# A threshold attention feeding a gated feed-forward: GpSimd's order in the lead-in, a later copy, and output pieces in the last slot

## The chip, the cores and the metric

The kernel runs on one core of a Trainium2 chip. The metric is the device time of one execution in microseconds; the median of three runs counts. The core has a tensor engine (PE, with its weight loads shown as PEld), a vector engine (DVE), a scalar engine (ACT), GpSimd (POOL) and a sync engine (SP). Each works through its own queue in order. SP, ACT and POOL can also issue DMA transfers.

## What is computed

```
# q, k, v: 8 images x 8 heads x 576 rows x 64
scores = q @ k.T / sqrt(64)
thresh = max(scores) - tau                      # per row, tau = 0.02
scores = where(scores >= thresh, scores, -1e9)
attn   = exp(scores - max(scores)); attn /= sum(attn) + 1e-9
x      = (attn @ v), heads side by side         # 4608 x 512
h      = x @ w_in                               # 512 -> 2048
g      = h * clip(h + 3, 0, 6) / 6
out    = g @ w_out                              # 2048 -> 512
```

## The kernel before

**Slots.** The attention is cut into 144 slots, 18 per image. A slot is 128 query rows of one pair of heads; slot numbers run through all images. For each slot:

- PE computes the scores of two slots at once in a `burst` (line 203), into the score columns of PSUM (`score_col`, line 196: banks 0 to 5; odd slots use banks 0 and 1, and 3 and 4, even slots 1 and 2, and 4 and 5). A burst can write only where the maxima of the two slots before have been read.
- DVE copies the scores to SBUF and takes the row maximum, one instruction per head (`sm_max`, line 225, instruction at line 233).
- POOL turns the maximum into a bias (`sm_bias`, line 241): one two-head instruction per slot, except in slots 0 and 1, where each head has its own.
- ACT applies the threshold (`sm_mask`, line 245, needs the bias) and the exponential with its row sum (`sm_exp`, line 250).
- DVE inverts the sum (`sm_recip`), POOL normalises into bf16 (`sm_norm`, line 257, two instructions per slot). This frees the slot's score tile in SBUF; there are five such tiles.
- The result is transposed on PE for the first ten slots (`pe_transpose`, with copies out by DVE, lines 281 and 282), and by DMA from SP for the others.

**Products and feed-forward.** `multiply(n)` (line 401) gives the products with v that are due in slot n and returns their copies out of PSUM (line 297, into `xT`; line 306, into `xR`). When the four products of a chunk are there, its feed-forward items go into the list `todo1`. An item (`mm1`, line 314) multiplies with `w_in`; then comes r = max(h + 3, 0) on ACT or DVE (lines 330 and 332) and the gate g on DVE (line 345). There are two r tiles. When a chunk's last item has been taken, its output tiles go into `todo2`, four pieces to a tile (`mm2_part`, line 352, four blocks of `w_out` each). A finished tile is copied out (`mm2_out`, line 359) and stored by four DMAs.

**The order.** It is written out by hand. The lead-in (`for n in range(0, N1, 2)`, line 476) takes slots 0 to 13 two at a time. One cycle issues: copies of the transposes, the burst for n + 2 and n + 3, the norms of the two slots before, the maximum of n + 2, the products with their copies, transposes, then the loads of slots n and n + 1 (`issues`), the maximum of n + 3, and ACT's exponentials and masks. In cycle n = 0 the loads of slot 0 are issued earlier, around the maximum of slot 2. The lists `issues` (lines 417 to 448) say which load is issued in which slot: pieces of `w_in` in 0, 0, 1, 1 and of `w_out` in 4, 6, 8, 10, all by POOL; slot 1 also has the k load of quad 2, by SP.

The main loop (line 518) takes slots 14 to 143 one at a time. In odd slots from 21 on `second()` (line 465) issues two pieces of an output tile on PE into bank 7 (`OB`), but not in the last slot, 143. Then the drain: `rest1` takes the items left, in banks 0, 3, 2, 5 in turn; `rest2` takes the pieces left, with banks 6 and 7 and copies out by ACT and DVE in turn (`count`); `last_tile` (line 571) does the last output tile in two halves with DMAs of their own.

What matters for the change: in cycle n = 12 the product copied is the fourth of the first chunk, and slot 14's item reads all four. The bias of a slot stands on POOL behind everything that was issued on POOL before it.

Of the kernel before, what the change touches and what calls it, by code (L numbers as in the profile page):

```python
# [20 lines left out]
def kernel(  # L21
# [10 lines left out]
    nc = tc.nc  # L32
# [7 lines left out]
    N1, N2 = 14, 21  # L40
    HB, OB = 6, 7
# [31 lines left out]
    issues = {}  # L73
    jobs = {}

    def at(when, n, job):
        when.setdefault(n, []).append(job)
# [90 lines left out]
    now = -1  # L168
# [14 lines left out]
    queue = []  # L183
    for b in range(B):
        for g, t in ((0, 0), (0, 1), (1, 0), (1, 1), (None, 4), (0, 2), (0, 3), (1, 2), (1, 3)):
            for i in range(2):
                sl = Slot()
# [8 lines left out]
    def score_col(n, a):  # L196
        return (512 - OWN if n % 2 else 1024 - P) + 1536 * a
# [27 lines left out]
    def sm_max(sl):  # L225
        sl.s = s_pool.tile([P, 2, S], F32, tag="s", name="s")
        sl.m = stat_pool.tile([P, 2], F32, tag="m", name="m")
        sl.bias = stat_pool.tile([P, 2], F32, tag="bias", name="bias")
        sl.rsum = stat_pool.tile([P, 2], F32, tag="rsum", name="rsum")
        sl.rinv = stat_pool.tile([P, 2], F32, tag="rinv", name="rinv")  # L230
        for i in range(2):
            c0 = score_col(sl.n, i)
            nc.vector.tensor_scalar(out=sl.s[:, i, :], in0=ps_flat[:, c0:c0 + S],  # L233
                                    scalar1=1.0, scalar2=None, op0=Alu.mult, op1=Alu.max,
                                    accum_out=sl.m[:, i:i + 1])
            if sl.n < 2:
                sm_bias(sl, slice(i, i + 1))
        if sl.n >= 2:
            sm_bias(sl)

    def sm_bias(sl, of=slice(0, 2)):
        nc.gpsimd.tensor_scalar(out=sl.bias[:, of], in0=sl.m[:, of], scalar1=-scale, scalar2=tau, op0=Alu.mult,  # L242
                                op1=Alu.add)
# [10 lines left out]
    def sm_recip(sl):  # L254
        nc.vector.reciprocal(out=sl.rinv[:], in_=sl.rsum[:])  # L255
# [18 lines left out]
    def pe_transpose(sl):  # L274
        i = sl.n % 2
        most = ps[:, (OB, HB)[i], :].bitcast(BF16).rearrange("p (c t) -> p c t", t=P)
        one = ps_flat[:, 1472 + 1536 * i:1536 + 1536 * i].bitcast(BF16)
        pn = sl.pn[:].rearrange("p a b -> p (a b)")
        for c in range(9):
            nc.tensor.transpose(most[:, c, :] if c < 8 else one, pn[:, c * P:(c + 1) * P], identb[:])  # L280
        return (lambda: nc.vector.tensor_copy(out=sl.dst[:, 8, :], in_=one),
                lambda: nc.vector.tensor_copy(out=sl.dst[:, 0:8, :], in_=most))
# [9 lines left out]
    def av_main(b, hp, chunk):  # L292
        if hp == chunk == 0:
            xT[b] = x_pool.tile([P, KI, 512], BF16, tag="xT", name="xT")
        pb = bank()
        av(pb, b, hp, pts[b, hp, chunk], slice(0, 256))
        return lambda: nc.vector.tensor_copy(out=xT[b][:, hp, 256 * chunk:256 * chunk + 256], in_=pb)  # L297

    def av_rest(b):
        pb = bank()  # L300
        for hp in range(NPAIR):
            av(pb[:, 64 * hp:64 * hp + 64], b, hp, ptr[b, hp % 2], slice(64 * (hp // 2), 64 * (hp // 2) + 64))
        if b % 2 == 0:
            xR[b // 2] = x_pool.tile([P, KI, P], BF16, tag="xR", name="xR")
        o0 = 64 * (b % 2)
        return lambda: nc.vector.tensor_copy(out=xR[b // 2][:, :, o0:o0 + 64],
                                             in_=pb.rearrange("p (a b) -> p a b", a=NPAIR))

    def half_columns(out, lhsT, rhs, start, stop):
        w = 64 if now < len(queue) - 1 else P  # L310
        for c in range(0, P, w):
            nc.tensor.matmul(out[c:c + w], lhsT[:, c:c + w], rhs, start=start, stop=stop)  # L312
# [39 lines left out]
    def mm2_part(mt, part, ob=OB):  # L352
        if part == 0:
            o_ps[0] = ps[:, ob, :]
        for ni in range(part * 4, part * 4 + 4):
            half_columns(o_ps[0], gbuf[:, ni, mt * P:(mt + 1) * P], w_out_sb[:, ni, :],
                         start=(ni == 0), stop=(ni == NI - 1))
# [15 lines left out]
    todo2 = []  # L373
# [7 lines left out]
    def whole(b, chunk):  # L381
        mt = 5 * (b % 2) + 2 * chunk
        items = [((b, ni, 256 * chunk), ()) for ni in range(0, NI, 2)]
        items[-1] = (items[-1][0], [(b // 2, mt + i, part) for i in range(2) for part in range(4)])
        return items

    def odd_items(b, halves):
        items = [((b, ni, None), ()) for half in halves for ni in (8 * half, 8 * half + 4)]
        if 1 in halves:
            items[-1] = (items[-1][0], [(b // 2, 4, part) for part in range(4)])  # L390
        return items
# [9 lines left out]
    def multiply(n):  # L401
        copies = []
        for b, hp, chunk in products.get(n, ()):
            if hp is None:
                copies.append(av_rest(b))
                if b % 2:
                    todo1.extend(odd_items(b, (0,) if b < B - 1 else (0, 1)))
                elif b:
                    todo1.extend(odd_items(b - 1, (1,)))
            else:  # L410
                copies.append(av_main(b, hp, chunk))
                if hp == NPAIR - 1:
                    todo1.extend(whole(b, chunk))
        return copies
# [16 lines left out]
    def v_pieces(b, slots):  # L431
        pieces = []

        def piece(i):
            if not pieces:
                pieces.extend(load_v(b))
            pieces[i]()

        for i, n in enumerate(slots):
            at(issues, n, lambda i=i: piece(i))  # L440

    v_pieces(0, (-1, -1, -1, -1, 0, 0, 0, 0))
    for b in range(1, B):
        v_pieces(b, (13, 14, 15, 16, 17, 18, 19, 20) if b == 1 else [(b - 1) * NSLOT + n for n in range(8, 24, 2)])
    for i, n in enumerate((0, 0, 1, 1)):
        at(issues, n, lambda i=i: load_w_in(i))
    for i, n in enumerate((4, 6, 8, 10)):
        at(issues, n, lambda i=i: load_w_out(i))
# [11 lines left out]
    for i in range(2):  # L460
        sm_max(queue[i])
# [2 lines left out]

    def second():
        nonlocal pieces, bb, mt, part
        pieces = 2 if now % 2 and todo2 and N2 <= now < len(queue) - 1 else 0
        for _ in range(pieces):
            bb, mt, part = todo2.pop(0)
            mm2_part(mt, part)  # L470

    pieces = bb = mt = part = 0
    waiting = [[], []]
# [2 lines left out]
    for n in range(0, N1, 2):  # L476
        now = n
        last = [queue[m] for m in (n - 2, n - 1) if m >= 0]
        ones, most = waiting
        for copy in ones:  # L480
            copy()
        for sl in last:
            sm_recip(sl)
        for copy in most[0:1]:
            copy()
        burst(n + 2, by=nc.sync)
        for copy in most[1:]:
            copy()
        for job in jobs.get(n, ()):
            job()  # L490
        for sl in last:
            sm_norm(sl)
        if n == 0:
            for issue in issues[0][:4]:
                issue()
        sm_max(queue[n + 2])
        if n == 0:
            for issue in issues[0][4:]:
                issue()
        warm_up({0: 15, 2: 8}.get(n, 3))  # L500
        for copy in multiply(n):
            copy()
        copies = [pe_transpose(sl) for sl in last if sl.on_chip]
        waiting = [[c[0] for c in copies], [c[1] for c in copies]]
        for issue in (issues.get(n, []) if n else []) + issues.get(n + 1, []):
            issue()
        sm_max(queue[n + 3])
        for m in (n, n + 1):
            for i in range(2):
                sm_exp(queue[m], i)  # L510
            for i in range(2):
                sm_mask(queue[m + 1], i)
# [5 lines left out]
    for n, sl in enumerate(queue[N1:], N1):  # L518
        now = n
        last = queue[n - 1:n]  # L520
# [33 lines left out]
        if part == 3:  # L554
            outs.append((bb, mt))
            part = 0
# [14 lines left out]
    def last_tile(mt):  # L571
        c = d_model // 2
        for half in range(2):
            o_half, columns = ps[:, (2, 5)[half], 0:c], slice(half * c, half * c + c)
            for ni in range(NI):
                nc.tensor.matmul(o_half, gbuf[:, ni, mt * P:(mt + 1) * P], w_out_sb[:, ni, columns],
                                 start=(ni == 0), stop=(ni == NI - 1))
            osb = o_pool.tile([P, d_model], F32, tag="osb", name="osb")
            nc.vector.tensor_scalar_mul(out=osb[:, 0:c], in0=o_half, scalar1=1.0 / 6.0)
            for i in range(4):  # L580
                (nc.scalar if i % 2 or half == 0 else nc.sync).dma_start(
                    out=rows_of(B - 1, 12 + i)[:, columns], in_=osb[R * i:R * i + R, 0:c])

    def rest1(item, then, on_act=True):
# [25 lines left out]
    now = len(queue)  # L610
# [42 lines left out]
```

## Time and profile before

| | |
|---|---|
| median of three runs | 501.12 us (500.88 to 501.15) |
| profiled execution, its own time | 501.12 us |
| its span | 499.4 us |
| POOL's norms (line 260) | 288, 748 ns each |
| maxima (line 233) | 288, 750 ns each |
| masks and exponentials (lines 247, 252) | 288 each, 763 and 671 ns |
| POOL's bias (line 242) | 146, 189 ns each |
| matmuls with `w_out` (line 312) | 1021, 379 ns each from issue to end |
| `w_in` loads | 4, 512 KB each, 8.8 us to landing |
| granted PE clock | full over almost the whole span |

How to read it: "busy" is time in which an engine had an instruction at work. PE's matmuls overlap, so their mean duration is longer than their distance. The chain that ended last is followed back from the last instruction. A bracket behind a row of the time line gives the engine's idle time before it and what ended it; a wait for several things is put down to the last of them. "x8" means that eight instructions were merged into one row.

### The profile page before, as it was taken

The numbers are of one execution on the slowest core, as the hardware profiler recorded it, in microseconds if no ns is written. First come the engines' busy times: TensorE is split into PE (matmuls) and PEld (weight loads), VectorE is DVE, ScalarE is ACT, GpSimd is POOL, SyncE is SP. The second block draws the span as 40 slices with busy tenths as digits, with TensorE's granted clock in tenths as the row PEclk, the third lists the DMA queues.
The fourth block names the chain that finished last, engine by engine and source line by source line (L and its number), as shares of the span: only waits on it lengthen the run. The fifth ranks groups of instructions, "written<-read, shape, count | busy, mean of one in ns | idle before, by whom it ended". The sixth has DMA issues, their size and how long they took to land.

```text
span 499.4 us, 17393 instructions
## 1 busy us (share of the span) xinstructions
PE 484.4 (97%) x6803; PEld 359.3 (72%) x6807; DVE 446.0 (89%) x1154; ACT 441.5 (88%) x949; POOL 294.1 (59%) x536
## 2 busy tenths in 40 slices
PE   8888999999999999999999999999999999998996
PEld 7767766777677776777677776777777776776474
DVE  6899998999999999999999999999999998887242
ACT  2899999999999999999999999999999999999132
POOL 3877786666666666666666666666666565554000
PEclk9999999999999999999999999999999999999999
DMA  7999998997999889998999798998999877766421
GB/s 213 177 200 190 150 173 168 223 121 165 174 176 190 119 174 184 216 145 176 166 205 178 129 173 179 220 149 154 181 187 191 123 144 116 151 118 118 91 59 42
DMA packets 192627, 79.98 MB, mean 160 GB/s; under 512 B 171169, under 2 KB 183841, under 8 KB 192545
## 3 DMA queue, kind: packets, MB, share of 16 engines
q1 hardware_dynamic: 175216, 55.27, 61.9%
q0 software_dynamic: 16896, 23.07, 24.0%
q8 instruction: 53, 0.87, 0.7%
q10 hardware_dynamic: 432, 0.52, 0.4%
q14 instruction: 30, 0.24, 0.2%
HBM read 36.70 MB, written 9.44 MB: 92 GB/s over the span
## 4 chain that ended last, share of the span: by engine, by line
PE 79%; ACT 12%; DVE 6%; issue 1%; POOL 1%; DMA 0%; SPq 0%; DVEq 0%
PE ps L312 45%; PE ps L219 26%; PE ps L289 6%; ACT s L247 5%; ACT s L252 5%; DVE s L233 4%; ACT r L330 1%; DVE g L345 1%; PE ps L155 1%; POOL w_in_sb L136 1%; DMA out_dram<-osb 0%; POOL pn L260 0%; DVE r L332 0%; DVE osb L364 0%; PE ps L159 0%
## 5 line engine op out<-in xcount | busy, mean ns | idle before, releaser
L260 POOL TENSOR_SCALAR pn<-s,rinv 128x576 bf16<-128x576 f32 x288 | 211.6, 748 | 15.1 <-issue 1.3
L233 DVE TENSOR_SCALAR_CACHE_REDUCE s<-ps 128x576 f32<-128x576 f32 x288 | 205.2, 750 | 16.3 <-PE ps L219 12.9
L247 ACT ACTIVATE s<-s,bias 128x576 f32<-128x576 f32 x288 | 205.8, 763 | 9.4 <-POOL bias L242 9.4
L252 ACT ACTIVATE s<-s 128x576 f32<-128x576 f32 x288 | 192.4, 671 | 0.0
L219 PE MATMUL ps<-kT,qT 32*128 32x128 f32 (+3 forms) x2560 | 167.3, 414 | 4.8 <-DVE s L233 4.4
L219 PEld LDWEIGHTS ps<-kT,qT 32*128 32x128 f32 (+1 forms) x2560 | 124.1, 174 | 49.2 <-DVE s L233 11.1
L312 PE MATMUL ps<-xT,w_in_sb 128*64 128x256 bf16 (+1 forms) x1936 | 132.9, 274 | 1.4 <-DVE g L345 1.4
L312 PE MATMUL ps<-w_out_sb,g 128*64 128x512 bf16 (+1 forms) x1021 | 130.7, 379 | 0.2
L312 PEld LDWEIGHTS <-w_in_sb 128*64 128x64 bf16 (+1 forms) x1936 | 105.7, 109 | 11.4 <-issue 4.2
L242 POOL TENSOR_SCALAR bias<-m 128x2 f32<-128x2 f32 (+1 forms) x146 | 27.6, 189 | 138.4 <-DVE rinv L255 123.6
L312 PEld LDWEIGHTS <-g 128*64 128x64 bf16 (+1 forms) x1024 | 61.6, 109 | 48.1 <-issue 0.2
L345 DVE SCALAR_TENSOR_TENSOR g<-r,ps 128x512 bf16<-128x512 f32 x128 | 87.4, 684 | 8.3 <-ACT r L330 4.4
L330 ACT ACTIVATE r<-ps,three 128x512 f32<-128x512 f32 x81 | 55.2, 686 | 25.4 <-PE ps L312 24.5
L252 ACT ACTIVATION_READ_ACCUMULATOR s<-s 128x1 f32 x288 | 54.8, 190 | 0.0
L289 PEld LDWEIGHTS <-v 128*64 128x64 bf16 x960 | 41.4, 111 | 16.0 <-issue 3.6
L289 PE MATMUL ps<-pT,v 128*64 128x256 bf16 x640 | 45.4, 273 | 1.6 <-DVE s L233 1.5
L332 DVE TENSOR_SCALAR r<-ps 128x512 f32<-128x512 f32 x63 | 43.3, 688 | 0.4
L119 POOL DMA_DIRECT2D v<-in_v_dram x64 | 36.9, 578 | 9.2 <-DVE kT L110 4.8
L364 DVE TENSOR_SCALAR osb<-ps 128x512 f32<-128x512 f32 x32 | 21.9, 684 | 8.5 <-PE ps L312 8.5
L297 DVE CAST xT<-ps 128x256 bf16<-128x256 f32 x64 | 26.0, 406 | 3.8 <-PE ps L289 3.4
L110 DVE STREAM_TRANSPOSE kT<-nk 128x320 f32<-128x320 f32 (+1 forms) x64 | 26.3, 451 | 0.9 <-DMA nk<-in_k_dram 0.9
L96 DVE STREAM_TRANSPOSE qT<-nq 128x640 f32<-128x640 f32 (+2 forms) x33 | 24.6, 749 | 0.6 <-DMA nq<-in_q_dram 0.6
(35 smaller groups left out, 173.5 us busy)
## 6 DMA issues: line engine op xcount, KB each, us to landing
out_dram<-osb SPq DMA_DIRECT2D x140, 64.0 KB, 2.5
nk<-in_k_dram POOLq DMA_DIRECT2D x12, 576.0 KB, 4.8
nq<-in_q_dram POOLq DMA_DIRECT2D x12, 576.0 KB, 4.9
v<-in_v_dram POOLq DMA_DIRECT2D x32, 80.0 KB, 4.1
v<-in_v_dram POOLq DMA_DIRECT2D x32, 64.0 KB, 3.1
w_in_sb<-in_moe_w_in_dram POOLq DMA_DIRECT2D x4, 512.0 KB, 8.8
w_out_sb<-in_moe_w_out_dram POOLq DMA_DIRECT2D x4, 512.0 KB, 7.0
pT<-pn SPq DMA_TRANSPOSE x120, 4.4
```

What stands on the lines that cost most here:

```text
L119: nc.gpsimd.dma_start(out=vsb[b % 2][32 * g:32 * g + 32].rearrange("p (hp a) c -> p a hp c", a=2)[:, a, :, c0 * D:(c0 + count) * D], in_=v ...
L219: mm = nc.tensor.matmul(ps_flat[rows, c0:c0 + w], qT[c:c + 32, j, q0:q0 + rows.stop - rows.start], kT[c:c + 32, j, k0:k0 + w], start=(j == ...
L233: nc.vector.tensor_scalar(out=sl.s[:, i, :], in0=ps_flat[:, c0:c0 + S], scalar1=1.0, scalar2=None, op0=Alu.mult, op1=Alu.max, accum_out=sl ...
L242: nc.gpsimd.tensor_scalar(out=sl.bias[:, of], in0=sl.m[:, of], scalar1=-scale, scalar2=tau, op0=Alu.mult, op1=Alu.add)
L247: nc.scalar.activation(out=s, in_=s, func=Act.Prelu, bias=sl.bias[:, i:i + 1], scale=scale, alpha=REJECT)
L252: nc.scalar.activation(out=s, in_=s, func=Act.Exp, accum_out=sl.rsum[:, i:i + 1])
L260: nc.gpsimd.tensor_scalar(out=pn[:, i, :], in0=sl.s[:, i, :], scalar1=sl.rinv[:, i:i + 1], scalar2=1.0, op0=Alu.mult, op1=Alu.mult)
L289: nc.tensor.matmul(pb[a * 64:(a + 1) * 64, :], vsb[b % 2][:, 2 * hp + a, u * D:(u + 1) * D], pT[:, block, cols], start=(c == 0), stop=(c = ...
L312: nc.tensor.matmul(out[c:c + w], lhsT[:, c:c + w], rhs, start=start, stop=stop)
L330: nc.scalar.activation(out=r, in_=hps, func=Act.Relu, bias=three[:])
L332: nc.vector.tensor_scalar(out=r, in0=hps, scalar1=3.0, scalar2=0.0, op0=Alu.add, op1=Alu.max)
L345: nc.vector.scalar_tensor_tensor(out=out, in0=r, scalar=6.0, in1=hps, op0=Alu.min, op1=Alu.mult)
```

## The change

Five edits:

1. The pieces of `w_in` are issued with slots 0, 1, 2 and 3, and in cycle n = 0 the loads of slot 1 are issued behind the maximum of slot 3. On POOL the order becomes: bias of slot 2, one piece, bias of slot 3, one piece, norms of slots 0 and 1, bias of slot 4, two pieces, bias of slot 5. The k load of quad 2 on SP moves with the loads of slot 1.
2. Slot 2 has a bias per head.
3. In a lead-in cycle in which no slot is transposed on PE (only n = 12 has both that and a product), the copy of the product comes behind the maximum of slot n + 3.
4. In slot 143 two pieces of the next output tile are issued, into bank 4, one of the score banks. The tile's other two pieces follow in the drain in the same bank. With it `count` starts at 0, so that the copies out of the drain change places between ACT and DVE.
5. Both halves of the last tile issue two DMAs from ACT and two from SP; before, the first half issued all four from ACT.

```diff
@@ sm_max
-            if sl.n < 2:
+            if sl.n < 3:
                 sm_bias(sl, slice(i, i + 1))
-        if sl.n >= 2:
+        if sl.n >= 3:
             sm_bias(sl)
@@
-    for i, n in enumerate((0, 0, 1, 1)):
+    for i, n in enumerate((0, 1, 2, 3)):
         at(issues, n, lambda i=i: load_w_in(i))
@@ second
-        pieces = 2 if now % 2 and todo2 and N2 <= now < len(queue) - 1 else 0
+        pieces = 2 if now % 2 and todo2 and now >= N2 else 0
         for _ in range(pieces):
             bb, mt, part = todo2.pop(0)
-            mm2_part(mt, part)
+            mm2_part(mt, part, ob=OB if now < len(queue) - 1 else 4)
@@ lead-in
-        for copy in multiply(n):
-            copy()
-        copies = [pe_transpose(sl) for sl in last if sl.on_chip]
+        products_out = multiply(n)
+        chip = [sl for sl in last if sl.on_chip]
+        if chip:
+            for copy in products_out:
+                copy()
+        copies = [pe_transpose(sl) for sl in chip]
         waiting = [[c[0] for c in copies], [c[1] for c in copies]]
-        for issue in (issues.get(n, []) if n else []) + issues.get(n + 1, []):
-            issue()
+        if n:
+            for issue in issues.get(n, []) + issues.get(n + 1, []):
+                issue()
         sm_max(queue[n + 3])
+        if n == 0:
+            for issue in issues[1]:
+                issue()
+        if not chip:
+            for copy in products_out:
+                copy()
@@ last_tile
-                (nc.scalar if i % 2 or half == 0 else nc.sync).dma_start(
+                (nc.scalar, nc.sync)[i % 2].dma_start(
```

## The prediction

> **What bounds the kernel now.** I read four views: the page's busy times and chain, the chain in order of time, the time line of the first 76 us, and the time line from 450 us.
>
> ```profile
> PE 484.4 (97%) x6803; PEld 359.3 (72%) x6807; DVE 446.0 (89%) x1154; ACT 441.5 (88%) x949; POOL 294.1 (59%) x536
> ...
> PE 79%; ACT 12%; DVE 6%; issue 1%; POOL 1%; DMA 0%; SPq 0%; DVEq 0%
> ```
>
> TensorE is busy for 484.4 of 499.4 us, and between 200 and 440 us the stretches show it without a gap. So time can come out only where PE idles or where its work can be moved into idle time: the lead-in (before 100 us PE idles 7.6 us) and the end.
>
> In the chain in order of time the lead-in runs through GpSimd:
>
> ```profile
> 14.42 1.44 DVE s L233 x4
> 16.98 2.24 POOL w_in_sb L136 x3
> 19.57 1.49 POOL pn L260 x2
> 21.08 1.46 DVE s L233 x4
> 22.80 1.44 ACT s L247 x2
> ```
>
> The time line says why (columns: start, duration, engine, line; the bracket is idle time and what ended it):
>
> ```profile
> 16.16 1.44 ACT L247 ACTIVATE s<-s,bias 128x576 f32<-128x576 f32 x2 [0.38 <-POOL bias L242]
> 16.18 3.04 POOL L136 DMA_DIRECT2D w_in_sb<-in_moe_w_in_dram  x4
> ...
> 19.51 1.44 ACT L247 ACTIVATE s<-s,bias 128x576 f32<-128x576 f32 x2 [0.59 <-POOL bias L242]
> 19.57 2.92 POOL L260 TENSOR_SCALAR pn<-s,rinv 128x576 bf16<-128x576 f32 x4
> ...
> 22.80 1.44 ACT L247 ACTIVATE s<-s,bias 128x576 f32<-128x576 f32 x2 [0.52 <-POOL bias L242]
> ```
>
> Four weight-load issues (3.04 us, 0.76 each) stand on POOL ahead of the bias of slot 3; the normalisations of slots 0 and 1 come after that, the bias of slot 4 after those. ACT waits 0.38 + 0.59 + 0.52 = 1.49 us.
>
> The next stretch is the hand-over from lead-in to main loop:
>
> ```profile
> 48.63 0.42 DVE L297 CAST xT<-ps 128x256 bf16<-128x256 f32 x1
> ...
> 49.39 1.07 PE L312 MATMUL ps<-xT,w_in_sb 128*64 128x256 bf16 x16
> ...
> 50.39 2.28 PE L219 MATMUL ps<-kT,qT 32*128 32x128 f32 x32
> ...
> 50.78 0.68 DVE L332 TENSOR_SCALAR r<-ps 128x512 f32<-128x512 f32 x1
> ...
> 52.91 0.72 DVE L233 TENSOR_SCALAR_CACHE_REDUCE s<-ps 128x576 f32<-128x576 f32 x1
> ```
>
> From 47.27 to 76.2 us DVE is idle only once (0.22 us at 61.39, waiting for ACT's r). So here DVE sets the pace, and what DVE has gained by slot 16 is what the rest can inherit. The end:
>
> ```profile
> 455.55 1.03 PE L312 MATMUL ps<-xT,w_in_sb 128*128 128x256 bf16 x8 [0.56 <-DVE g L345]
> ...
> 457.45 1.03 PE L312 MATMUL ps<-xT,w_in_sb 128*128 128x256 bf16 x8 [0.87 <-DVE g L345]
> ...
> 461.78 13.98 PE L312 MATMUL ps<-w_out_sb,g 128*128 128x512 bf16 x63
> ...
> 494.30 2.71 ACTq L581 DMA_DIRECT2D out_dram<-osb  x6
> ...
> 496.04 0.79 SPq L581 DMA_DIRECT2D out_dram<-osb  x2
> ```
>
> PE idles 0.56 + 0.87 = 1.43 us for free banks, then runs almost without a gap to 495.55; that run sets the end.
>
> **Part 1, POOL's order in the lead-in (weight loads, bias per head).** Removed: three issues between the biases of slots 2 and 3. Added: one one-head bias (0.19 us, the row at 10.11). By rows: the first head's maximum of slot 2 is done at 15.16, its bias at 15.45, ACT is free at 15.68 (13.01 mask plus 2.67 a slot), so that mask starts 0.48 earlier. Then one issue (16.18 to 16.94); bias of slot 3 behind its maximum (17.19) at 17.29; second issue to 18.26; the four normalisations 18.35 to 21.27; bias of slot 4 to 21.55, its mask at 21.57 instead of 22.80: ACT gains 1.23. The last two issues run to 23.1, bias of slot 5 to 23.36 (not needed before 24.24), and the normalisations of slots 2 and 3 start at 23.46, as before (23.44): they cover nothing and cost nothing. The key load of quad 2, moved with the issues on SP, passes only a no-op that waits for the burst; it was issued at 13.34 and is read at 24.50. The weights are first read at 49.39, and a load lands in 8.8 us (the page), so their lateness costs nothing.
>
> What DVE gains is less. Its maximum of slot 5 waited for the buffer that slot 0's normalisation frees (0.09 us at 21.08), and its copies waited 0.38 for PE transposes behind slot 1's. Freed of both, slot 5's maximum ends at 22.35, the burst for slots 6 and 7 ends at 22.41 + 2.23 = 24.64, and slot 6's maximum starts 0.16 later, at 24.80, instead of 25.34: **0.54 us**. From there the lead-in is a loop of two maxima, one copy and a burst, 5.57 us a cycle (36.13, 41.70, 47.27) against ACT's 5.33, so ACT's lead shrinks to DVE's and 0.54 arrives at slot 14 (46.73).
>
> **Part 2, the later copy.** The xT copy goes behind the maxima of slot 15. Nothing is added on DVE, but this copy is the fourth of the four that the first hidden-layer item reads. Without the shift it would end at 50.40, with it at 49.86, instead of 49.05. PE starts that item at 48.85, runs 6 of 16 matmuls, and then waits until 49.92. Behind it in PE's queue stands the burst for slots 16 and 17, and DVE's r. The 10 left take 10 x 1.0/16 = 0.63, so the burst starts at 50.55 (before: 50.39) and ends at 52.78; slot 16's maximum follows 0.17 later, at **52.95 against 52.91**. The 0.54 is spent, plus 0.04. DVE waits about 0.5 for r meanwhile. ACT still leads by 0.5 to 0.9, which takes the 0.22 at 61.39. Head: 0.54 - 0.58 + 0.22 = **0.18 us**. Bounds: if the wait cost nothing, 0.54 + 0.22 = 0.76; if DVE's 0.54 never came, the copy would end at 50.40, the burst start at 51.09 and slot 16 at 53.49, a loss of 0.58 - 0.22 = 0.36. I take 0.18, since both ends need a row to be wrong.
>
> A rule of the Trainium skill speaks against this part ("PSUM — Partial Sum Buffer", section "Engine vs sequencer instructions"): matmuls start and complete in program order. In this trace PE's weight loads idle 0.74 and 1.04 us around the two waits of 0.56 and 0.87, so nothing ran past them. By the rule the head is 0.18; if the burst could pass the waiting item, 0.76.
>
> **Part 3, two pieces in the last slot.** Eight matmuls of 512 columns, 13.98 / 64 = 0.218 us each, 1.75 us, leave the run at 461.78 and go behind slot 143's item, at about 452.2. Bank 4 was last read by slot 143's maximum, to 450.95: no wait. The next three items then start at 454.0, 454.9 and 455.8 and end before ACT's r reach them (456.01, 456.66, 457.50, with ACT held by the exps to 456.1); the fourth starts at 456.7 (its bank is free at 455.50), the fifth at 457.6 (457.40). So both idle times are filled and the r-g chain isn't late. The xR items end at 461.94 - 1.43 + 1.75 = 462.26, with 1.75 less to follow: **1.43 us** gained. An item alone lasts 1.03, in a row 0.85 to 0.9 (3.50 us for 33 weight loads at 451.31), so up to 0.35 more can come with the restart: 1.78. I take **1.6**. If the pieces delayed the r-g chain after all, this falls towards 0. The copies out change engines (last full tile on DVE, 0.69 instead of ACT's 0.60), off PE's path: the copy after it waits for PE until 495.55.
>
> **Part 4, the last DMAs.** ACT issued six, ending at 497.01; SP's two ended at 496.83. Two and two, behind a copy done at 496.01, end on both at about 496.85: **0.16 us**. SP has the four issues of the tile before (to 494.4) and then two of the first half (to 495.4) ahead, so it is free. Bounds 0 and 0.2.
>
> Sum: 0.18 + 1.6 + 0.16 = 1.94. The profiled execution took 501.12 us (span 499.4 and 1.7 around it), which is also the median. **499.2 us**.
>
> **Rivals.**
> - *The copy's wait is harmless.* For it: DVE has other work just behind the copy (two reciprocals, the xR copy). Against: r and the burst both come behind that item. Head 0.76, total 2.5: 498.6.
> - *The pieces are hidden anyway.* If the tail were set by ACT's r and DVE's g, whose pairs follow each other at 1.50 us from 456.01 to 461.2, filling PE's gap would bring nothing. Against: from 461.78 PE has 34 us of work left and DVE waits 5.3 us for it. 0.18 + 0.16: 500.8.
> - *Slower: a wait that comes back with every image.* In the main loop PE waits for maxima where an image's products change bank (0.36 at 95.50, 0.67 at 102.08), and later no more. If the new phase of DVE against PE brought back about 0.5 us in each of the last six images, 3.0 us would be added: 501.12 - 1.94 + 3.0 = 502.2. It decides from 2.9 us on. Against: everything behind slot 24 moves together.
>
> **How the numbers follow.** Forecast 0.66, harmless copy 0.18, hidden pieces 0.11, recurring wait 0.05. A change of 0.2% (1.0 us) is about what a measurement of this kernel tells from none. The first two cases are faster, 0.84; the third is within, 0.11; the fourth slower, 0.05. Range: the best bounds of all parts give 501.12 - 0.76 - 1.78 - 0.2 = 498.4; the worst of head and end with the lower tail give 501.12 + 0.36 - 1.43 = 500.05, so 500.1.
>
> **What would show it.** Masks of slots 2, 3, 4 at about 15.7, 18.4 and 21.6, with hardly a wait on a bias left; slot 6's maximum near 24.8 and slot 14's near 46.7; then a PE wait on the xT copy in the item near 49.3, DVE idle about 0.5 ahead of r, and slot 16's maximum at 52.9; slot 24's about 0.2 before 76.44. At the end no idle of 0.56 and 0.87 in PE, 56 matmuls in the run from about 462, and the last issues of ACT and SP side by side. Wrong would be: slot 16 at 52.4 (copy harmless), or new waits on g between 453 and 462 (pieces in the way).

## The result, and the profile after

The changed kernel takes 499.12 us (median of six runs, 498.97 to 499.35) against 501.01 for the kernel before in the same comparison: ratio 0.9963, 95% interval 0.995 to 0.9976. The forecast was 499.2. The profiled execution took 499.35 us with a span of 497.57; the one of before 501.12 with 499.35. One of the five executions of e10_copy_between, a kernel of the experiments below, was disturbed (524.56 us at a granted clock of 0.943), and its median is that of the other four.

The busy times on the page have hardly moved; the span around them is shorter:

```profile
PE 484.7 (97%) x6807; PEld 359.7 (72%) x6807; DVE 445.9 (90%) x1154; ACT 441.5 (89%) x949; POOL 294.4 (59%) x537
```

So the gain is idle time, as it had to be. The time line of the lead-in (start, duration, engine, line; the bracket is idle time before and what ended it):

```profile
15.77 1.43 ACT L247 ACTIVATE s<-s,bias 128x576 f32<-128x576 f32 x2
...
16.27 0.80 POOL L136 DMA_DIRECT2D w_in_sb<-in_moe_w_in_dram  x1
...
18.43 1.43 ACT L247 ACTIVATE s<-s,bias 128x576 f32<-128x576 f32 x2
18.48 2.92 POOL L260 TENSOR_SCALAR pn<-s,rinv 128x576 bf16<-128x576 f32 x4
...
21.71 1.44 ACT L247 ACTIVATE s<-s,bias 128x576 f32<-128x576 f32 x2 [0.51 <-POOL bias L242]
...
24.88 0.76 DVE L233 TENSOR_SCALAR_CACHE_REDUCE s<-ps 128x576 f32<-128x576 f32 x1
```

The masks of slots 2, 3 and 4 start at 15.77, 18.43 and 21.71 (16.16, 19.51 and 22.80 before), slot 6's maximum at 24.88 (25.34). The norms start 1.1 us earlier. The hand-over to the main loop, in the same view:

```profile
48.94 0.52 PE L312 MATMUL ps<-xT,w_in_sb 128*64 128x256 bf16 x6
...
49.53 0.42 DVE L297 CAST xT<-ps 128x256 bf16<-128x256 f32 x1
...
50.01 0.74 PE L312 MATMUL ps<-xT,w_in_sb 128*64 128x256 bf16 x10 [0.54 <-DVE xT L297]
...
50.67 2.23 PE L219 MATMUL ps<-kT,qT 32*128 32x128 f32 x32
50.78 0.69 DVE L332 TENSOR_SCALAR r<-ps 128x512 f32<-128x512 f32 x1 [0.37 <-PE ps L312]
...
53.08 0.76 DVE L233 TENSOR_SCALAR_CACHE_REDUCE s<-ps 128x576 f32<-128x576 f32 x1
```

The item of slot 14 is cut in two, six matmuls and ten, with 0.54 us between them in which PE waits for the copy. The burst for slots 16 and 17 stands behind the ten. DVE, with a lead of half a microsecond, waits 0.37 for that item, and slot 16's maximum is no earlier than before (52.91). The end:

```profile
452.06 1.89 PE L312 MATMUL ps<-w_out_sb,g 128*128 128x512 bf16 x8
...
453.78 4.56 PE L312 MATMUL ps<-xT,w_in_sb 128*128 128x256 bf16 x40
...
458.18 3.62 PE L312 MATMUL ps<-w_in_sb,xR 128*128 128x512 bf16 x16
...
461.63 12.25 PE L312 MATMUL ps<-w_out_sb,g 128*128 128x512 bf16 x56
...
492.43 2.60 ACTq L591 DMA_DIRECT2D out_dram<-osb  x4
492.76 2.19 SPq L591 DMA_DIRECT2D out_dram<-osb  x4
```

The waits of 0.56 and 0.87 are gone, eight matmuls stand at 452.06, and the run from 461.63 has 56 and lasts 12.25 instead of 13.98.

### The profile page after: what moved, and what is told of

It reads as the page before. It is cut to its first block, busy times and chain, and to the rows that moved or that the text cites. A ratio compares the mean times of both kernels' runs of the same rounds, so it can differ in the third digit from the quotient of the medians.

```text
span 497.6 us, 17398 instructions
## 1 busy us (share of the span) xinstructions
PE 484.7 (97%) x6807; PEld 359.7 (72%) x6807; DVE 445.9 (90%) x1154; ACT 441.5 (89%) x949; POOL 294.4 (59%) x537
## 4 chain that ended last, share of the span: by engine, by line
PE 79%; DVE 5%; DMA 2%; issue 2%; POOL 1%; ACT 0%; SPq 0%; POOLq 0%; DVEq 0%
PE ps L312 47%; PE ps L219 25%; PE ps L289 7%; DVE s L233 3%; DMA pT<-pn 2%; POOL pn L260 1%; DVE g L345 1%; ACT r L330 0%; DVE osb L364 0%; DMA out_dram<-osb 0%; DVE r L332 0%; DVE pR L282 0%; SPq L379 0%; POOL v L119 0%; DVE xT L297 0%
```

## The experiments

The first maximum starts at a different time in each profile (8.74 to 9.34 us in the twelve of this study). It waits for the first loads, which no edit here touches. So places in the lead-in are counted from it, and the end from slot 24's maximum. "Slot 16" is the start of that slot's maximum; "end" is the distance from slot 24's maximum to the last attention products (at 475.68 before).

| kernel | edits | median us | ratio to before, 95% interval | slot 6 | slot 16 | slot 24 | end |
|---|---|---|---|---|---|---|---|
| before | none | 501.01 | | 16.10 | 43.67 | 67.20 | 399.24 |
| changed | 1 to 5 | 499.12 | 0.9963 (0.995 to 0.9976) | 15.54 | 43.74 | 66.95 | 397.52 |
| e1_pieces | 4 | 499.27 | 0.997 (0.9959 to 0.9981) | 16.07 | 43.66 | 67.18 | 397.52 |
| e2_lead | 1, 2 | 499.97 | 0.9985 (0.9976 to 0.9993) | 15.55 | 43.13 | 66.32 | 399.25 |
| e3_no_late_copy | 1, 2, 4, 5 | 498.37 | 0.9952 (0.9939 to 0.9964) | 15.55 | 43.14 | 66.33 | 397.52 |
| e4_late_copy | 3 | 501.23 | 1.0009 (1.0 to 1.0018) | 16.08 | 44.28 | 67.50 | 399.26 |
| e6_loads | 1 | 500.17 | 0.9986 (0.9977 to 0.9995) | 15.55 | 43.12 | 66.31 | 399.25 |
| e7_bias | 2 | 500.90 | 1.0001 (0.9992 to 1.001) | 16.08 | 43.66 | 67.19 | 399.24 |
| e10_copy_between | all, copy half-way | 498.33 | 0.995 (0.9936 to 0.9964) | 15.55 | 43.13 | 66.31 | 397.53 |
| e11_two_edits | 1, 4 | 498.59 | 0.9955 (0.9942 to 0.9969) | 15.55 | 43.13 | 66.31 | 397.52 |
| e8_one_piece | 4, one piece | 499.97, one run | | 16.09 | 43.67 | 67.20 | 398.39 |
| e9_four_pieces | 4, four pieces | 499.06, one run | | 16.07 | 43.65 | 67.16 | 397.49 |

In the comparisons with e1 to e4, and with e6, e7, e10 and e11, the kernel before took 500.85 and 500.84; beside e8 and e9 one run took 501.07. The places repeat to about 0.03 us from profile to profile, much finer than the times, so the readings rest on them. Each kernel has one profile. All times are within 0.6% of each other; e4's interval and e7's reach 1.0, so their times alone tell nothing.

**Pieces alone** (edit 4 on the kernel before):

```diff
-        pieces = 2 if now % 2 and todo2 and N2 <= now < len(queue) - 1 else 0
+        pieces = 2 if now % 2 and todo2 and now >= N2 else 0
...
-            mm2_part(mt, part)
+            mm2_part(mt, part, ob=OB if now < len(queue) - 1 else 4)
```

> Edit 4 alone (two pieces of the next output tile in slot 143, bank 4) on the kernel before. Theory (PE sets the end and its two idle times of 0.56 and 0.87 us are filled): nothing moves before 450 us, the two waits on g vanish, the run of w_out matmuls from about 462 has 56 instead of 64, the last products start at 474.0 instead of 475.68, time 1.7 us below the kernel before, about 499.3. Rival (the r-g chain sets the end, the pieces are hidden anyway): the items behind the pieces wait for g instead, the last products start within 0.3 of 475.68 and the time is that of the kernel before.

End 397.52 instead of 399.24: 1.72 us, with nothing moved before 450. The time is 499.27, 1.58 below the kernel before. The pieces aren't hidden.

**Lead-in order alone** (edits 1 and 2), the copy left in its place:

```diff
-            if sl.n < 2:
+            if sl.n < 3:
...
-        if sl.n >= 2:
+        if sl.n >= 3:
...
-    for i, n in enumerate((0, 0, 1, 1)):
+    for i, n in enumerate((0, 1, 2, 3)):
...
-        for issue in (issues.get(n, []) if n else []) + issues.get(n + 1, []):
-            issue()
+        if n:
+            for issue in issues.get(n, []) + issues.get(n + 1, []):
+                issue()
         sm_max(queue[n + 3])
+        if n == 0:
+            for issue in issues[1]:
+                issue()
```

> Edits 1 and 2 alone (order of the weight loads on POOL, bias per head in slot 2), the xT copy where it was. Theory (the late copy spends what the lead-in gains): maximum of slot 6 about 0.54 earlier than the 25.34 of before, slot 14 at 46.7, then no PE wait on the xT copy, r of slot 14 at 50.2 to 50.3, slot 16 at 52.4 instead of 52.91, slot 24 0.7 earlier than 76.44, time 0.75 below the kernel before, about 500.3. Rival (the late copy is harmless, the lead is lost elsewhere): slot 16 back at 52.9 to 53.0 and slot 24 only 0.1 to 0.2 earlier, time 500.8 to 500.9.

Slot 16 is 0.54 earlier, slot 24 0.88, the time 0.88 below the kernel before. The late copy isn't harmless.

**The changed kernel without the late copy:**

```diff
-        products_out = multiply(n)
-        chip = [sl for sl in last if sl.on_chip]
-        if chip:
-            for copy in products_out:
-                copy()
...
+        for copy in multiply(n):
+            copy()
...
-        if not chip:
-            for copy in products_out:
-                copy()
```

> The changed kernel without edit 3: the copy of the last lead-in cycle stands between the maxima again. Theory: the PE wait of 0.54 in slot 14's item and DVE's 0.37 ahead of r vanish, slot 16 at 52.4 to 52.5 instead of 53.08, slot 24 0.5 to 0.6 ahead of 76.29, time 0.55 below the changed kernel, about 498.55 (2.5 below the kernel before). Rival (late copy harmless): slot 24 and time as in the changed kernel, 499.1.

Its time line, to be held against that of the changed kernel above:

```profile
47.59 0.42 DVE L297 CAST xT<-ps 128x256 bf16<-128x256 f32 x1
...
48.36 1.07 PE L312 MATMUL ps<-xT,w_in_sb 128*64 128x256 bf16 x16
...
49.36 2.29 PE L219 MATMUL ps<-kT,qT 32*128 32x128 f32 x32
49.74 0.68 DVE L332 TENSOR_SCALAR r<-ps 128x512 f32<-128x512 f32 x1
...
51.88 0.72 DVE L233 TENSOR_SCALAR_CACHE_REDUCE s<-ps 128x576 f32<-128x576 f32 x1
```

The item is whole again, the burst follows it, and r has no wait before it. The first maximum was at 8.74 in this profile, 0.60 earlier than in the changed kernel; with that taken out, slot 16 is still 0.60 earlier (43.14 against 43.74), and slot 24 0.62. The two kernels weren't timed in one comparison; 498.37 against 499.12 is a difference of two medians, 0.75, and the places say that 0.62 of it is the copy.

**Late copy alone** (edit 3 on the kernel before):

```diff
-        for copy in multiply(n):
-            copy()
+        products_out = multiply(n)
+        chip = [sl for sl in last if sl.on_chip]
+        if chip:
+            for copy in products_out:
+                copy()
...
         sm_max(queue[n + 3])
+        if not chip:
+            for copy in products_out:
+                copy()
```

> Edit 3 alone on the kernel before. Theory: the xT copy ends at 50.40 instead of 49.05, PE waits about 1 us for it in slot 14's item, the burst behind starts at 51.1 instead of 50.39, slot 16 at 53.5 instead of 52.91, DVE then makes up the 0.22 it waited for ACT's r, slot 24 0.36 later than 76.44, time 0.36 above the kernel before, about 501.4. Rival (harmless): slot 24 within 0.1 of 76.44, time 501.0; a gain would show slot 24 earlier.

```profile
49.13 0.52 PE L312 MATMUL ps<-xT,w_in_sb 128*64 128x256 bf16 x6
...
49.72 0.42 DVE L297 CAST xT<-ps 128x256 bf16<-128x256 f32 x1
...
50.20 0.74 PE L312 MATMUL ps<-xT,w_in_sb 128*64 128x256 bf16 x10 [0.54 <-DVE xT L297]
```

Slot 16 is 0.61 later and slot 24 0.30, the time 0.38 above the kernel before, about as expected, though the interval reaches 1.0. The expected wait of about 1 us is a miss: it is 0.54, as in the changed kernel. The item stands on PE behind the products, which wait for slot 14's maximum (0.51 us in both profiles), and the copy stands on DVE behind slot 15's, so the two shift together whether the lead is there or not.

**Which of the two lead-in edits?** Edit 1 alone, then edit 2 alone (of the diff of e2_lead the last two parts, and the first two):

> Edit 1 alone (weight loads behind the biases of slots 2 to 4), slot 2 with one bias for both heads. Theory (DVE's lead comes from the norms that no longer stand behind four issues; the bias per head only moves ACT, which is not the pace): slot 2's mask waits 0.38 as before, slot 6's maximum 0.55 earlier counted from the first maximum, slot 24's 0.85 to 0.9 earlier, time as edits 1 and 2 together, 0.75 to 0.9 below the kernel before, 500.0 to 500.1. Rival (the two edits share the gain): slot 24 clearly less than 0.8 earlier.

> Edit 2 alone (bias per head in slot 2). Theory: slot 2's mask 0.4 to 0.5 earlier, slot 3's still waits behind the four issues and starts where it did, so nothing else moves: slot 24 within 0.05 of before (counted from the first maximum), time that of the kernel before. Rival (ACT is the pace of the lead-in): slot 24 0.3 to 0.5 earlier.

Masks and loads on the time line, first with edit 1 alone:

```profile
15.84 1.44 ACT L247 ACTIVATE s<-s,bias 128x576 f32<-128x576 f32 x2 [0.38 <-POOL bias L242]
...
15.87 0.80 POOL L136 DMA_DIRECT2D w_in_sb<-in_moe_w_in_dram  x1
...
17.23 0.80 POOL L136 DMA_DIRECT2D w_in_sb<-in_moe_w_in_dram  x1
...
18.52 1.43 ACT L247 ACTIVATE s<-s,bias 128x576 f32<-128x576 f32 x2
...
21.30 1.44 ACT L247 ACTIVATE s<-s,bias 128x576 f32<-128x576 f32 x2
```

and with edit 2 alone:

```profile
15.30 1.43 ACT L247 ACTIVATE s<-s,bias 128x576 f32<-128x576 f32 x2
...
15.80 3.04 POOL L136 DMA_DIRECT2D w_in_sb<-in_moe_w_in_dram  x4
...
19.13 1.44 ACT L247 ACTIVATE s<-s,bias 128x576 f32<-128x576 f32 x2 [1.07 <-POOL bias L242]
...
22.42 1.44 ACT L247 ACTIVATE s<-s,bias 128x576 f32<-128x576 f32 x2 [0.52 <-POOL bias L242]
```

With edit 1 alone slot 2's mask waits 0.38, and slot 24 is 0.89 earlier all the same. With edit 2 alone slot 2's mask starts without a wait, and slot 3's then waits 1.07 instead of 0.59: the half microsecond has only gone one slot down, and slot 24 stays at 67.19. The bias per head is worth nothing here; by the places the order of the loads is worth all. By the times it is a little less clear: edit 1 alone is 0.67 below the kernel before (500.17, where 500.0 to 500.1 was expected), both edits 0.88, with intervals that overlap almost wholly.

Edit 1 gains in two steps: slot 6 and slot 16 are 0.55 earlier, slot 24 0.89. Two pairs of rows of the kernel before show what it removes:

```profile
22.55 0.45 PE L280 MATMUL ps<-identb,pn 128*128 128x128 bf16 x5 [0.33 <-POOL pn L260]
...
23.04 0.23 DVE L281 COPY pT<-ps 128x128 bf16<-128x128 bf16 x1 [0.38 <-PE ps L280]
...
61.08 0.09 DVE L233 DVE_READ_ACCUMULATOR s<-ps 128x1 f32 x1
...
61.39 0.69 DVE L345 SCALAR_TENSOR_TENSOR g<-r,ps 128x512 bf16<-128x512 f32 x1 [0.22 <-ACT r L330]
```

First, PE's transposes wait for the norms, and DVE's copies for the transposes; with edit 1 alone neither row has a wait. Second, DVE waits for ACT's r. In the kernel before, ACT shows no idle time from slot 4's mask, which waited 0.52 for its bias, up to that r. With edit 1 alone the mask of slot 4 starts 1.19 earlier and that r 0.96 earlier (50.48 against 51.44 us after the first maximum), and DVE's wait is gone.

**The copy half-way**, between the two heads of slot 15's maximum, in the changed kernel:

```diff
-    def sm_max(sl):
+    def sm_max(sl, between=()):
...
+            if i == 0:
+                for copy in between:
+                    copy()
...
-        sm_max(queue[n + 3])
+        sm_max(queue[n + 3], () if chip else products_out)
...
-        if not chip:
-            for copy in products_out:
-                copy()
```

> The changed kernel with the copy of the last lead-in cycle between the two heads of slot 15's maximum, 0.68 us earlier than in the changed kernel and as much later than in the kernel before. Theory (it costs only because PE waits for the copy): PE reaches the seventh matmul of slot 14's item at about the time the copy is done, so the wait of 0.54 falls to nothing or at most 0.1, slot 16 as without the late copy (43.1 to 43.2 after the first maximum, against 43.74), time 498.4 to 498.5. Rival (a later place on DVE costs by itself, in proportion): half of the loss stays, slot 16 at 43.45, time 498.75.

```profile
48.47 1.12 PE L315 MATMUL ps<-xT,w_in_sb 128*64 128x256 bf16 x16
```

Slot 16 at 43.13, time 498.33: the item is whole and none of the loss is left, though the copy is half as late on DVE as in the changed kernel. So a later place on DVE costs nothing by itself here; the cost begins where the copy ends later than PE comes to the seventh matmul.

**Edits 1 and 4 alone:**

> Edits 1 and 4 alone: loads behind the biases, two pieces in slot 143; no bias per head, no late copy, DMAs of the last tile as before. Theory (these two carry all of the gain): 0.87 in the lead-in and 1.72 at the end, time 2.5 below the kernel before, 498.4, as the changed kernel without the late copy. Rival (bias per head or the last DMAs carry 0.2 or more): 498.6 or above.

Slot 24 at 66.31, end 397.52, time 498.59 (498.52 to 498.73). The time comes out where the rival had it (498.6), not at 498.4, but in its places it is e3_no_late_copy. The two profiled spans, 496.74 and 496.34, differ by 0.40, and the first maximum is at 9.13 in one and 8.74 in the other: 0.39 of the 0.40, before anything that the edits touch. Whether the 0.2 us between the medians comes from there too, one profile of each can't show.

**One piece and four** instead of two in slot 143:

```diff
+        pieces = (1 if now == len(queue) - 1 else 2) if now % 2 and todo2 and now >= N2 else 0
...
```

This is the line for one piece; for four it has 4 in place of 1, and the bank is as in edit 4.

> Edit 4 with one piece instead of two in slot 143 (the run that follows has 60 w_out matmuls). Theory (only PE's idle time can be gained): the 0.87 us of one piece fills the first wait (0.56) and no more; the second, 0.87 for the bank that g frees at 457.40, stays; the xR items start where they did, so the gain is the piece's own 0.87: last products 398.35 to 398.4 us after slot 24's maximum (399.24 without, 397.52 with two). Rival (work moved ahead is gained in full whatever the idle time): the same here, so this run alone does not tell; it is read together with four pieces.

> Edit 4 with four pieces, a whole tile, in slot 143 (48 w_out matmuls in the run that follows). Theory (only PE's idle time can be gained, and two pieces fill it): PE runs without a wait, the xR items start 1.75 us later than with two pieces, and the last products come where they come with two, 397.5 us after slot 24's maximum, 397.4 to 397.6. Rival (work moved ahead is gained in full): 395.8. Third possibility (the r-g chain gets late behind four pieces): later than 397.7, with waits for g in front of the items.

PE's time line with one piece, and below it with four:

```profile
451.81 1.03 PE L312 MATMUL ps<-w_out_sb,g 128*128 128x512 bf16 x3
452.68 3.66 PE L312 MATMUL ps<-xT,w_in_sb 128*128 128x256 bf16 x32
457.07 1.03 PE L312 MATMUL ps<-xT,w_in_sb 128*128 128x256 bf16 x8 [0.74 <-DVE g L345]
457.94 3.62 PE L312 MATMUL ps<-w_in_sb,xR 128*128 128x512 bf16 x15
```

```profile
451.85 3.62 PE L312 MATMUL ps<-w_out_sb,g 128*128 128x512 bf16 x15
455.30 4.53 PE L312 MATMUL ps<-xT,w_in_sb 128*128 128x256 bf16 x40
459.67 3.62 PE L312 MATMUL ps<-w_in_sb,xR 128*128 128x512 bf16 x15
463.12 3.19 PE L312 MATMUL ps<-w_out_sb,g 128*128 128x512 bf16 x14
```

With one piece the first wait is gone and 0.74 of the second is left; end 398.39, a gain of 0.85. With four there is no wait either, but the xR items start 1.70 later than with two (383.59 after slot 24's maximum against 381.89), and the end is 397.49. The gain grows 0, 0.85, 1.72, 1.75 with 0, 1, 2 and 4 pieces: what is moved ahead counts only as far as there is idle time to take it. Four pieces of 16 x 0.218 = 3.49 us less 1.70 of delay have filled 1.79 us. The kernel before shows that room in the idle time of its weight loads at the two places:

```profile
455.55 0.86 PEld L312 LDWEIGHTS <-w_in_sb 128*128 128x128 bf16 x8 [0.74 <-issue]
...
457.45 0.75 PEld L312 LDWEIGHTS <-w_in_sb 128*128 128x128 bf16 x7 [1.04 <-issue]
```

## Why the prediction was right, point by point

- **POOL's order.** The masks were forecast at 15.7, 18.4 and 21.6 and came at 15.77, 18.43 and 21.71, with the first maximum 0.10 later than before. DVE's lead at slot 6 is 16.10 - 15.54 = 0.56 (forecast 0.54), and it keeps: at slot 14 it is 0.55. "Hardly a wait on a bias left" was a miss: slot 4's mask still waits 0.51.
- **ACT set the pace once.** Its waits for biases fell from 1.49 to 0.51 us between slots 2 and 4. Up to slot 16 that is worth nothing, since the loop of maxima, copy and burst is the pace, as the 5.57 against 5.33 us a cycle said; ACT's wait at slot 2 can stay or go (e6, e7). But ACT's lead did not shrink to DVE's, as the prediction had it: at slot 14's mask it is still 0.97 us (40.21 us after the first maximum before, 39.24 in the changed kernel), and it is this lead that removes the wait for r.
- **The late copy.** Forecast: 0.58 lost up to slot 16. Shown: 0.60 (43.74 against 43.14) and, on the kernel before, 0.61. The mechanism is the one named, though DVE waits 0.37 for r where about 0.5 was forecast. PE waits 0.54 at the seventh matmul, the burst stands behind, and the rule quoted from the Trainium skill ("PSUM — Partial Sum Buffer", "Engine vs sequencer instructions") holds in this trace: no burst starts before the ten matmuls that wait. On the kernel before the copy costs only 0.30 at slot 24, because DVE, being late, no longer waits for ACT's r.
- **The wait for ACT's r, "0.22", was mis-sized.** From slot 18's maximum to slot 20's it was 6.15 us before, and is 5.84 in the changed kernel and in e2: 0.31. (DVE is idle again from 75.93, not 76.2, for the 0.51 us before slot 24's maximum, with the change as without.) The row's idle time ends at 61.39, but it starts at the end of an accumulator read (61.08 to 61.17) which the next instruction overlaps when it needn't wait: in the changed kernel both start at 61.27. The wait cost 0.31, not 0.22. So the head gave 0.25 (67.20 to 66.95) where 0.18 was forecast, and 0.88 without the late copy where 0.76 was.
- **The two pieces.** Forecast 1.6, between 1.43 and 1.78; shown 1.72. The step "the xR items end at 462.26" was wrong: they start 381.89 after slot 24's maximum, as before (381.88). The idle time of the matmul rows, 1.43, was the wrong measure, since it counts from the modelled end of the last matmul. The weight loads' idle time at the same two places, 0.74 + 1.04 = 1.78, is the room that was there: two pieces (1.75) fit into it, four filled 1.79, and with one piece 0.91 of it is left (idle before the weight load at 457.07). The prediction had both bounds and took 1.6 between them, without a row that said which was right.
- **The last DMAs, "0.16", were mis-sized.** From PE's last matmul to the end of the last issue it was 1.46 us before and is 1.35; but to the end of the span it was 3.80 and is 3.89. With edit 4 and the old DMAs (e1, e11) these are 1.57 and 3.89 to 3.91; with the old DMAs and no pieces (before, e2, e4, e6, e7) the second is 3.79 to 3.82. So the DMA edit brings the last issue forward by 0.22 and the end by 0.02. From the landing of the last store to the end of the span it takes 1.29 to 1.30 us in the three profiles with the DMA edit (changed, e3, e10) and 1.17 to 1.18 in the other nine; why is open. The 0.1 by which e1 and e11 are longer is not explained by the copy of the tile before, which went to DVE (0.69 instead of 0.60 us on ACT): with four pieces it is on DVE too, and the end is 3.82. In e1, e8 and e11 one of ACT's last issues takes 0.52 to 0.54 us, in the others none takes over 0.45; that too stays open.
- **The sum.** In the profiles: 0.25 + 1.72 - 0.09 (end) - 0.10 (first maximum later) = 1.78, which is the difference of the spans, 499.35 - 497.57. Forecast were 0.18 + 1.6 + 0.16 = 1.94. Two terms came out higher, by 0.07 and 0.12, and the one that fell away came out 0.25 lower. That 499.2 lies within 0.1 us of the measured 499.12 is therefore in part luck.
- **The rivals.** A harmless copy is refuted by e2, e3 and e4. Hidden pieces are refuted by e1 and by the series of one, two and four. A wait that comes back with every image did not come: from slot 24 to the xR items it is 381.88 to 381.90 us in all profiles but that with four pieces, whatever the lead.

The best version found is the changed kernel without the late copy, or with the copy half-way: 498.37 and 498.33 us.

## What to carry to other kernels

An instruction issued ahead of others on the same queue can be paid by everybody who waits for one of those; here the place of four load issues on POOL cost 0.9 us. Of these, 0.55 came through the norms behind them, which no wait of ACT names, and the other 0.34, 0.31 of it between slots 18 and 20, through ACT, which stayed late from slot 4's mask on until DVE had to wait for it. ACT's wait for slot 2's bias was worth nothing. Before a copy is moved back, ask who reads it and what stands behind that reader in its queue: two of this change's parts give 2.6 us by their places (0.89 and 1.72), and a third took 0.6 back. Work moved ahead was worth the idle time that it filled, measured at the weight loads, and no more.

## What the runs showed that was not expected

The places are far more repeatable than the times. Eleven of the twelve profiles have the same distance from slot 24 to the xR items to 0.02 us in 382, while the start of the first maximum, which waits for the first loads, lies anywhere between 8.74 and 9.34 us. Much of the spread of the times (500.62 to 501.17 for the kernel before in one comparison) can come from there; that wasn't tried by itself.
